# Loading half of the spectral weights two rows per partition, w_r on even and w_i on odd partitions

## The chip, the cores and the metric

The kernel runs on one core of a Trainium2 chip. The metric is the device time of one execution in microseconds (us), as the median of several runs. A run on one core counts as slow when it took over 1.5% longer than the fastest run of the same kernel. In the lines of the profile PE is TensorE's products and PEld its loading of the stationary operand, DVE is VectorE, ACT ScalarE, POOL GpSimd and SP SyncE; L12 is line 12 of the kernel. The granted clock is the share of TensorE's full speed that it was allowed in a stretch.

## The reference, cut to what matters

Attention with a decay gives x (8 batches, 576 positions, d = 512). A spectral layer follows; its weights are most of the bytes that the kernel reads (2 x 64 x 512 x 512 numbers of 4 bytes, 134 MB of the 164 MB that the profile counts).

```python
def _moe_ref(x, w_r, w_i, w_ch):            # x: (8, 576, 512); w_r, w_i: (64, 512, 512)
    X = np.fft.rfft(x, axis=1)
    Xr, Xi = np.real(X[:, :64]), np.imag(X[:, :64])
    Yr = einsum('bmd,mde->bme', Xr, w_r) - einsum('bmd,mde->bme', Xi, w_i)
    Yi = einsum('bmd,mde->bme', Xr, w_i) + einsum('bmd,mde->bme', Xi, w_r)
    ...                                      # inverse transform gives y
    u = x + y
    return u + np.maximum(u @ w_ch, 0.0)
```

## The kernel before: the parts that matter

The 64 weight tiles of 1 MiB (as written, in two-byte numbers) pass through a ring of nine buffers. All these loads are issued by GpSimd (POOL), in program order (POOL's timeline shows them so), and convert from four-byte to two-byte numbers on the way (the page counts 163.73 MB read from HBM in all, and 85.34 MB, as written, for this queue). Tiles 0 to 31 hold four modes of 128 rows of d, one row per partition; tiles 32 to 63 hold two modes of 256 rows, two rows per partition.

```python
def emit_w_load(n):
    dc, g = tile_of(n)
    if n < NTH:                                              # tiles 0..31
        wb = wpool.tile([128, 2, MG, D], BF16, tag="wb", name="wb")
        for t, src in enumerate((moe_w_r, moe_w_i)):
            pool_dma(wb[:, t, :, :],
                     src[g*MG:(g+1)*MG, dc*128:(dc+1)*128, :].rearrange("m p e -> p m e"))
    else:                                                    # tiles 32..63
        wb = wpool.tile([128, 2, M2, 2 * D], BF16, tag="wb", name="wb")
        ...  # "m (p r) e -> p m (r e)", r=2: two rows of d per partition
```

`emit_modes` multiplies a tile with X: per mode and block of 128 output columns, w_r meets the columns (Xr, Xi) and w_i meets (-Xi, Xr). These 16 columns lie side by side in `XT3[:, m, c0:c0+16]`. `emit_dft` makes XT3 from x, after each pair of batches:

```python
px = psT.tile([128, NM, 2], F32, ...)                        # 5 products into px
nc.vector.tensor_copy(_strided(XT3[:, 0, B + b:...], [[3*B, NM], [B, 2]]), px)
nc.scalar.mul(XT3[:, :, b:b+1], px[:, :, 1:2], -1.0)
```

The main loop over steps s (one head of two batches each) prefetches nine tiles, and from s = 9 on multiplies tiles, each of which frees a ring buffer and lets one more load be issued:

```python
if h == 0 and pr + STG - 1 < NPR: emit_loads(pr + STG - 1)   # k, q, v of a later pair
if s < 10 and nload < min(NRING, 3 + 3*s//4): next_w()
if s == 10: pool_dma(wch[:], ...)                            # w_ch, 0.5 MiB
...
if s >= 1 and h == 0: emit_dft(pr - 1)
if s > B:
    while nmode < (s - B) * NTH // (NS - B):
        emit_modes(nmode); nmode += 1; next_w()
```

The softmax here doesn't subtract the row's maximum and nothing guards it: scores larger than these inputs give would overflow.

## Time and profile before

| | before |
|---|---|
| time | 448.64 us (448.20 to 449.03, 3 runs) |
| profiled execution | 446.5 us |
| weights (and w_ch) in 1024-byte packets | 33,280 |
| weights in 2048-byte packets | 16,384 |
| last weight load lands | 405.3 us |

From the page of the kernel before: the span, the rows of the 40 slices for DMA (busy tenths of 16 engines, then GB/s as written), the packets, and the chain of waits by engine and by line.

```profile
span 446.5 us, 11102 instructions
...
DMA  8999999999999999999999999999999999991698
GB/s 203 206 233 233 234 234 233 152 233 206 233 234 207 234 216 224 233 211 229 231 210 235 211 212 211 211 211 211 211 211 211 211 211 211 211 196 28 225 362 296
DMA packets 66431, 97.25 MB, mean 218 GB/s; under 512 B 3376, under 2 KB 44848, under 8 KB 66384
...
DMA 58%; PE 18%; DVE 7%; ACT 7%; issue 3%; POOL 1%; SPq 1%; DVEq 0%; ACTq 0%; POOLq 0%
```

The queue is full from the second slice to the 36th, but for the eighth (152 GB/s, around 80 to 90 us). This hole can be seen closer in stretches of the kernel before (columns: stretch, its length, busy time of each engine with the count of instructions, granted clock, DMA share, GB/s), together with two stretches in which weights alone load:

```profile
78.00:80.00 2.00, 1.90 (x45) 1.70 (x45) 1.90 (x7) 1.62 (x4) 0.00 (x0) 1.00 1.01 168
80.00:81.00 1.00, 1.00 (x35) 0.97 (x31) 0.73 (x2) 0.04 (x1) 0.07 (x1) 1.00 0.28 51
81.00:82.00 1.00, 1.00 (x17) 0.65 (x15) 1.00 (x3) 1.00 (x2) 0.96 (x2) 1.00 0.11 27
82.00:83.00 1.00, 1.00 (x18) 0.76 (x17) 1.00 (x2) 1.00 (x2) 1.00 (x2) 1.00 0.63 48
...
101.00:109.00 8.00, 7.95 (x161) 6.12 (x159) 5.73 (x18) 6.48 (x10) 2.68 (x4) 0.96 1.24 206
...
300.00:400.00 100.00, 51.91 (x941) 35.70 (x939) 16.38 (x44) 12.97 (x23) 25.73 (x37) 0.69 1.12 211
```

The DMA share falls to 0.11 at 81 us. Small packets fill the queue at a share of 1.24 and large ones at 1.12: the share is the time that the packets took, summed, over the time of 16 engines, so a share above 1 only says that packets overlap, and the lower share in the second half is not an idle queue. What counts is bytes per time, and there the two forms differ by little (206 and 211 GB/s).

Why the hole is there is read from POOL's order of instructions in the kernel before (start, duration, line, what; in brackets how long POOL was idle before, and what ended that):

```profile
64.76 0.74 POOL L88 DMA_DIRECT2D wb<-in_moe_w_i_dram  x1 [1.75 <-DMA wb<-in_moe_w_r_dram]
80.93 0.74 POOL L88 DMA_DIRECT2D wb<-in_moe_w_r_dram  x1 [15.43 <-PE tp L437]
```

After nine tiles the ring is full, and POOL issues nothing for 15 us: the loads of k, q, v and w_ch that stand behind the blocked tile in program order are issued after it, at 82.43 to 84.85 us. The releaser named is TensorE's instruction that came last by the profile; in the chain of waits of the kernel before (start, duration, what) it is the products of the first tile, `A`, that end just before:

```profile
76.36 1.30 DVE XT L581 x2
...
79.87 0.76 PE A L138 x31
80.63 0.31 PE tp L437 x5
80.94 0.73 POOL wb L88
```

Two groups of the kernel before, by shape (count, busy us, mean ns, idle time before), that the change replaces in the first half:

```profile
L581 DVE CAST XT<-px 128x128 bf16<-128x128 f32 x32 | 21.0, 805 | 8.6 <-PE px L571 8.6
L585 ACT ACTIVATE XT<-px 128x64 bf16<-128x64 f32 x32 | 14.4, 466 | 18.9 <-DVE XT L581 18.0
```

(The busy time, 21.0 us over 32, is 0.66 us apiece: neighbours overlap a little.)

### The profile page before, as it was taken

Reading aid. Unit: us, or ns where it says so; the run is one execution under the profiler, and the core shown is the slowest. Engines: PE = TensorE matmul, PEld = TensorE weight load, DVE = VectorE, ACT = ScalarE, POOL = GpSimd, SP = SyncE. Lnnn points to the kernel's source line nnn. Section 1 sums busy time; section 2 is a strip of 40 time slices with the busy share of each in tenths; the row PEclk is TensorE's granted clock in tenths of the full one; section 3 lists DMA queues with packets and bytes.
Section 4 is the critical chain, followed back from the end, with each engine's and each line's share of the span. In section 5 each row is a group of like instructions: output and inputs, shape, how many; then the busy total and the mean of one; then the engine's idle time right before and its main releaser. Section 6 shows DMA issues by size and latency. Waiting matters only on the chain.

```text
span 446.5 us, 11102 instructions
## 1 busy us (share of the span) xinstructions
PE 327.1 (73%) x4791; PEld 222.6 (50%) x4791; DVE 237.3 (53%) x602; ACT 202.4 (45%) x296; POOL 146.1 (33%) x194
## 2 busy tenths in 40 slices
PE   2388888989788788768597969999822238527993
PEld 1255555766566566556465746656612224323441
DVE  5768888776676546656377664223300002103894
ACT  3378888647567454664446533443200002102442
POOL 7333330534343323323333223232322323200661
PEclk9999999959599555897769578999955558856998
DMA  8999999999999999999999999999999999991698
GB/s 203 206 233 233 234 234 233 152 233 206 233 234 207 234 216 224 233 211 229 231 210 235 211 212 211 211 211 211 211 211 211 211 211 211 211 196 28 225 362 296
DMA packets 66431, 97.25 MB, mean 218 GB/s; under 512 B 3376, under 2 KB 44848, under 8 KB 66384
## 3 DMA queue, kind: packets, MB, share of 16 engines
q0 software_dynamic: 62480, 85.34, 103.3%
q1 hardware_dynamic: 3824, 11.09, 6.9%
q8 instruction: 37, 0.61, 0.5%
q10 hardware_dynamic: 80, 0.13, 0.1%
q14 instruction: 10, 0.08, 0.0%
HBM read 163.73 MB, written 9.44 MB: 388 GB/s over the span
## 4 chain that ended last, share of the span: by engine, by line
DMA 58%; PE 18%; DVE 7%; ACT 7%; issue 3%; POOL 1%; SPq 1%; DVEq 0%; ACTq 0%; POOLq 0%
DMA wb<-in_moe_w_i_dram 30%; DMA stk<-in_k_dram 13%; DMA stq<-in_q_dram 11%; ACT E L496 4%; DMA wb<-in_moe_w_r_dram 3%; PE tp L437 3%; PE pav L534 3%; PE pxw L680 3%; PE ps L489 3%; PE A L138 2%; DVE XT L581 2%; PE vp L461 1%; DVE uo L821 1%; PE ptr L669 1%; ACT KT L450 1%
## 5 line engine op out<-in xcount | busy, mean ns | idle before, releaser
L496 ACT ACTIVATE E<-ps 128x1024 bf16<-128x1024 f32 (+1 forms) x128 | 104.5, 859 | 39.3 <-PE ps L489 27.2
L138 PE MATMUL A<-XT,wb 128*128 128x16 bf16 x2048 | 71.6, 172 | 56.8 <-DMA wb<-in_moe_w_i_dram 35.0
L138 PEld LDWEIGHTS <-wb 128*128 128x128 bf16 x2048 | 64.0, 100 | 72.6 <-DMA wb<-in_moe_w_i_dram 38.2
L88 POOL DMA_DIRECT2D wb<-in_moe_w_r_dram x65 | 47.5, 731 | 134.7 <-PE A L138 30.4
L88 POOL DMA_DIRECT2D wb<-in_moe_w_i_dram x65 | 47.1, 725 | 78.2 <-DMA wb<-in_moe_w_i_dram 45.1
L489 PE MATMUL ps<-QTs,KT 64*128 64x64 bf16 (+4 forms) x384 | 57.5, 319 | 6.1 <-ACT E L496 5.9
L534 PE MATMUL pav<-va,E 128*128 128x65 bf16 (+1 forms) x1088 | 55.9, 210 | 4.3 <-DVE x_all L556 2.6
L534 PEld LDWEIGHTS <-E 128*128 128x128 bf16 (+1 forms) x1088 | 45.1, 114 | 15.8 <-issue 5.6
L153 DVE TENSOR_TENSOR YT<-A,Yacc 128x128 bf16<-128x128 f32 x24 | 8.9, 369 | 77.2 <-PE A L138 77.2
L511 DVE TENSOR_TENSOR E<-E,trimask 128x256 bf16<-128x256 bf16 (+2 forms) x128 | 38.2, 317 | 6.8 <-ACT E L496 6.4
L450 ACT COPY KT<-tp 128x640 bf16<-128x640 bf16 (+1 forms) x32 | 22.1, 745 | 26.6 <-PE tp L437 26.4
L687 ACT CAST XW<-pxw 128x512 bf16<-128x512 f32 x36 | 20.3, 587 | 29.8 <-PE pxw L680 25.1
L680 PE MATMUL pxw<-wch,yy 128*128 128x512 bf16 x144 | 33.5, 382 | 0.0
L699 ACT CAST yy<-pyw 128x512 bf16<-128x512 f32 x8 | 4.7, 586 | 60.7 <-PE pyw L692 60.7
L437 PE MATMUL tp<-ident_bf,kb 128*128 128x128 bf16 x144 | 16.1, 269 | 19.1 <-DVE kb L421 19.1
L556 DVE TENSOR_TENSOR x_all<-pav,rcp 128x384 bf16<-128x384 f32 x64 | 29.2, 456 | 0.9
L454 ACT COPY VT<-tp 128x640 bf16<-128x640 bf16 (+1 forms) x32 | 22.5, 753 | 12.6 <-PE tp L437 12.4
L489 PEld LDWEIGHTS <-KT 64*128 64x128 bf16 x384 | 18.1, 98 | 19.8 <-issue 11.6
L828 POOL TENSOR_TENSOR uo<-uo 128x1024 f32<-128x1024 f32 x7 | 16.5, 2359 | 29.3 <-DVE uo L821 25.5
L581 DVE CAST XT<-px 128x128 bf16<-128x128 f32 x32 | 21.0, 805 | 8.6 <-PE px L571 8.6
L425 DVE TENSOR_TENSOR vb<-stv,wdec 128x1152 bf16<-128x1152 f32 x16 | 21.6, 1351 | 5.4 <-PE tp L437 4.7
L452 DVE COPY QTs<-tp 128x640 bf16<-128x640 bf16 (+1 forms) x32 | 23.3, 767 | 0.8 <-PE tp L437 0.8
(108 smaller groups left out, 439.4 us busy)
## 6 DMA issues: line engine op xcount, KB each, us to landing
wb<-in_moe_w_r_dram POOLq DMA_DIRECT2D x63, 512.0 KB, 17.6
wb<-in_moe_w_i_dram POOLq DMA_DIRECT2D x63, 512.0 KB, 18.1
out_dram<-uo SPq DMA_DIRECT2D x16, 512.0 KB, 3.7
stv<-in_v_dram POOLq DMA_DIRECT2D x14, 576.0 KB, 15.6
stk<-in_k_dram POOLq DMA_DIRECT2D x16, 288.0 KB, 15.3
stq<-in_q_dram POOLq DMA_DIRECT2D x16, 288.0 KB, 15.3
stv<-in_v_dram SPq DMA_DIRECT2D x2, 576.0 KB, 6.1
out_dram<-uo SPq DMA_DIRECT2D x7, 128.0 KB, 3.9
```

The lines of the kernel that those rows point to most:

```text
L88: tc.keep_in_program_order(nc.gpsimd.dma_start(dst, src))
L138: nc.tensor.matmul(A[:, eb, mi, :], lhsT=wb[:, t, mi, r * D + eb * 128 : r * D + (eb + 1) * 128], rhs=XT3[:, m, c0 : c0 + 2 * B], start=(i ...
L437: nc.tensor.transpose(tp[:, r - r0, :, :].rearrange("c h p -> c (h p)"), sb[:, r, :, :].rearrange("p b d -> p (b d)"), ident_bf[:, :],)
L450: nc.scalar.copy(rows(KTs[pr % 2][:, :, 0:S]), tv)
L452: nc.vector.tensor_copy(rows(QT[pr][:, :, :]), tv)
L489: nc.tensor.matmul(ps[:, b, o : o + n], lhsT=KTs[pr % 2][bs, h, jb * 128 : (jb + 1) * 128], rhs=QT[pr][bs, h, jb * 128 + c0 : jb * 128 + c ...
L496: nc.scalar.activation(E[:, :, piece * 512 : piece * 512 + w], ps[:, :, 0:w], ACT.Exp, scale=scale,)
L511: nc.vector.tensor_tensor(dg, dg, tr, ALU.mult)
L534: nc.tensor.matmul(pav[64 * half : 64 * half + w, slot, :], lhsT=E[:, b, c : c + (w - 1) * st + 1 : st], rhs=va[:, jb, b, :], start=(n == ...
L556: nc.vector.tensor_tensor(xo, pi, ri, ALU.mult)
L581: nc.vector.tensor_copy(_strided(XT3[:, 0, B + b : B + b + 1], [[3 * B, NM], [B, 2]]), px[:, :, :],)
L680: nc.tensor.matmul(pxw[:, :], lhsT=xT[:, eb, i * 128 : (i + 1) * 128], rhs=wch[:, eb, :], start=(eb == 0), stop=(eb == NDC - 1),)
```

## The change

The intent is longer packets for the first half's weights as well: 2048 bytes as written, 4 KB as read. Rows 2p and 2p+1 of d then lie in one partition, so X must lie the same way. Both w_r and w_i still have to share a tile of 128 rows of d. So w_r is put on the even partitions and w_i on the odd ones, and X is dealt to match: a copy T holds (-Xi, Xr, Xi), and four products with selection matrices put (Xr, Xi) of row 2p+r on partition 2p and (-Xi, Xr) on partition 2p+1. The number of products with the weights stays the same (2048), since each now sums over both w_r and w_i.

```diff
 # emit_w_load, n < NTH
-            wb = wpool.tile([128, 2, MG, D], BF16, tag="wb", name="wb")
+            wb = wpool.tile([128, MG, 2 * D], BF16, tag="wb", name="wb")
             for t, src in enumerate((moe_w_r, moe_w_i)):
                 pool_dma(
-                    wb[:, t, :, :],
+                    wb[t:128:2, :, :],
                     src[g * MG : (g + 1) * MG, dc * 128 : (dc + 1) * 128, :
-                    ].rearrange("m p e -> p m e"),
+                    ].rearrange("m (p r) e -> p m (r e)", r=2),
                 )
 # emit_modes, n < NTH: lhsT = wb[:, mi, r*D+es : r*D+es+128], rhs = XT3s[dc][:, r, :, m]
 # setup: two selection matrices, basis stored as [.., 2, NM] (a permuted copy)
+        for r, t in enumerate(sel):
+            nc.vector.memset(t[:, :], 0.0)
+            nc.vector.tensor_copy(_strided(t[:, 1:2], [[2, 64]]), _strided(ident_bf[:, r:r+1], [[2, 64]]))
 # emit_dft, dc < 2
+                        nc.vector.tensor_copy(T[:, 1:3, b % 2, :], px[:, :, :])
+                        nc.scalar.mul(T[:, 0, b % 2, :], px[:, 1, :], -1.0)
+                px2 = psT.tile([128, 2, 4 * NM], F32, tag="tr", name="px2")
+                for r in (0, 1):
+                    for t in (0, 1):
+                        nc.tensor.matmul(px2[:, r, :], lhsT=sel[r][:, 1 - t : 129 - t],
+                            rhs=T[:, 1 - t : 3 - t, :, :].rearrange("p c b m -> p (c b m)"),
+                            start=(t == 0), stop=(t == 1), skip_group_check=True)
+                nc.vector.tensor_copy(_strided(XT[:, 0, 2*bp, 0:1], [[2*B*NM, 2], [B*NM, 2], [1, 2*NM]]),
+                    px2[:, :, :].rearrange("p r (c n) -> p r c n", c=2))
```

(Lines are joined and cut; the XT copies of the second half only change the order in which they read.)

More of the change, by code (lines that the diff above doesn't have):

```diff
@@ L69 @@
     wch = const.tile([128, NDC, D], BF16, name="wch")
-    bas = const.tile([128, NSB + 1, NM, 2], BF16, name="bas")
+    bas = const.tile([128, NSB + 1, 2, NM], BF16, name="bas")
+    sel = [const.tile([128, 130], BF16, name=f"sel{r}") for r in range(2)]
     BI = const.tile([128, SP], BF16, name="BI")
@@ L128, in emit_modes @@
         if n < NTH:
-            terms = [(XT3s[dc], 0, t, c0) for t, c0 in ((0, B), (1, 0))]
+            terms = [
+                (lambda mi, es, r=r: wb[:, mi, r * D + es : r * D + es + 128],
+                 lambda m, r=r: XT3s[dc][:, r, :, m])
+                for r in (0, 1)
+            ]
         else:
             terms = [
-                (XT3s[2 + r], r, t, c0) for t, c0 in ((0, B), (1, 0)) for r in (0, 1)
+                (lambda mi, es, t=t, r=r: wb[:, t, mi, r * D + es : r * D + es + 128],
+                 lambda m, c0=c0, r=r: XT3s[2 + r][:, m, c0 : c0 + 2 * B])
+                for t, c0 in ((0, B), (1, 0))
+                for r in (0, 1)
             ]
@@ L136, in emit_modes @@
             for eb in range(NDC):
-                for i, (XT3, r, t, c0) in enumerate(terms):
+                for i, (w_of, x_of) in enumerate(terms):
                     nc.tensor.matmul(
                         A[:, eb, mi, :],
-                        lhsT=wb[:, t, mi, r * D + eb * 128 : r * D + (eb + 1) * 128],
-                        rhs=XT3[:, m, c0 : c0 + 2 * B],
+                        lhsT=w_of(mi, eb * 128),
+                        rhs=x_of(m),
                         start=(i == 0),
@@ L171 @@
         nrm = actx.enter_context(tc.tile_pool(name="nrm", bufs=4))
+        tpl = actx.enter_context(tc.tile_pool(name="tpl", bufs=1))
         ssb = actx.enter_context(tc.tile_pool(name="ssb", bufs=1))
@@ L277 @@
         nc.vector.tensor_copy(ident_f[:, :], ident_bf[:, :])
+        for r, t in enumerate(sel):
+            nc.vector.memset(t[:, :], 0.0)
+            nc.vector.tensor_copy(
+                _strided(t[:, 1:2], [[2, 64]]), _strided(ident_bf[:, r : r + 1], [[2, 64]])
+            )
         for t in VTs:
@@ L360, in emit_basis @@
             NB1 = NSB + 1
-            s_f = ssb.tile([128, NB1], F32, name="s_f")
+            s_f = scratch(128, NB1)
             nc.vector.tensor_copy(s_f[:], s_i[:])
-            m_f = ssb.tile([128, NM], F32, name="m_f")
+            m_f = scratch(128, NM)
             nc.vector.tensor_copy(m_f[:], m_i[:])
@@ L394, in emit_basis @@
             nc.vector.memset(Zt[0:64, 5, :, :], 0.0)
-            nc.vector.tensor_copy(bas[:, :, :, :], Zt[:, :, :, :])
+            nc.vector.tensor_copy(
+                bas[:, :, :, :], Zt[:, :, :, :].rearrange("p s m t -> p s t m")
+            )
             coef = ssb.tile([128, 1], F32, name="coef")
@@ L562, in emit_dft @@
             forms = [(dc, dc * 128, 1)] if dc < 2 else [(2, 256, 2), (3, 257, 2)]
+            if dc < 2:
+                if bp == 0:
+                    XT3s[dc] = xtpool.tile(
+                        [128, 2, 2 * B, NM], BF16, tag="XT3", name=f"XT{dc}"
+                    )
+                T = tpl.tile([128, 3, 2, NM], BF16, tag="T", name="T")
             for b in (2 * bp, 2 * bp + 1):
                 for c, d0, st in forms:
-                    if b == 0:
+                    if b == 0 and dc == 3:
                         XT3s[c] = xtpool.tile(
@@ L568, in emit_dft @@
                         )
-                    px = psT.tile([128, NM, 2], F32, tag="tr", name="px")
+                    px = psT.tile([128, 2, NM], F32, tag="tr", name="px")
                     for sb in range(NSB):
@@ L579, in emit_dft @@
                         )
+                    if dc < 2:
+                        nc.vector.tensor_copy(T[:, 1:3, b % 2, :], px[:, :, :])
+                        nc.scalar.mul(T[:, 0, b % 2, :], px[:, 1, :], -1.0)
+                        continue
                     XT3 = XT3s[c]
                     nc.vector.tensor_copy(
-                        _strided(XT3[:, 0, B + b : B + b + 1], [[3 * B, NM], [B, 2]]),
+                        _strided(XT3[:, 0, B + b : B + b + 1], [[B, 2], [3 * B, NM]]),
                         px[:, :, :],
                     )
-                    nc.scalar.mul(XT3[:, :, b : b + 1], px[:, :, 1:2], -1.0)
+                    nc.scalar.mul(
+                        _strided(XT3[:, 0, b : b + 1], [[3 * B, NM]]), px[:, 1, :], -1.0
+                    )
+            if dc < 2:
+                px2 = psT.tile([128, 2, 4 * NM], F32, tag="tr", name="px2")
+                for r in (0, 1):
+                    for t in (0, 1):
+                        nc.tensor.matmul(
+                            px2[:, r, :],
+                            lhsT=sel[r][:, 1 - t : 129 - t],
+                            rhs=T[:, 1 - t : 3 - t, :, :].rearrange(
+                                "p c b m -> p (c b m)"
+                            ),
+                            start=(t == 0),
+                            stop=(t == 1),
+                            skip_group_check=True,
+                        )
+                XT = XT3s[dc]
+                nc.vector.tensor_copy(
+                    _strided(
+                        XT[:, 0, 2 * bp, 0:1], [[2 * B * NM, 2], [B * NM, 2], [1, 2 * NM]]
+                    ),
+                    px2[:, :, :].rearrange("p r (c n) -> p r c n", c=2),
+                )
         NS = len(steps)
```

## The prediction

> **What bounds the kernel now.** The DMA queue that carries the weights. In the chain of waits 58% of the span is DMA, 30% of it w_i loads; in the 40-slice table the DMA row is at 8 or 9 until 405 us. Only the first 8 us and a hole at 80 to 83 us are not full (windows of 1 us: DMA share 0.28, 0.11, 0.63, against 1.2 when full). The 42 us tail after 405 us is output work that the change does not touch.
>
> **What the change saves.** The loads of d's first half (32 tiles of 1 MiB as written in bf16) go in 1024-byte packets; those of the second half already in 2048-byte ones. The packet records, where weights alone move, give 199.7 packets/us for the small (101 to 109 and 150 to 158 us) and 102.3 packets/us for the large (300 to 400 us). One MiB takes 5.13 us or 5.00 us: 0.124 us a tile, 4.0 us for 32 tiles if the new loads reach the second half's rate.
>
> **How much lies on the critical path.** Nine of the 32 tiles are loaded before the hole at 80 us. There the ring is full, POOL waits 15 us, and the queue runs dry until the first tile's products (PE A, in the chain at 77.7 to 80.6) free a slot. The chain from 20 to 82 us is compute (ACT E, PE, DVE). Faster loads there only widen the hole. 23 tiles remain: 2.9 us.
>
> **What the change adds, on that early compute chain.** Per pair of batches of the first half: two contiguous DVE copies px to T, estimated at 0.35 us from the BI copy of that size (0.347), instead of XT copies of 0.72; two ACT products of about 0.3 instead of 0.46; then four selection products of 256 columns (estimated 0.6 us with latency, from 128-column products at 0.25 and 512-column ones at 0.4) and one DVE copy of 128x512 out of PSUM, about 0.65 (from 0.56 for 128x384). [...] the last pair stands in the chain just before tile 0's products. I estimate 0.8 us there, 0.5 us for the earlier pairs and the prologue (two selection matrices, a permuted basis copy), and 0.2 us for products whose 16 columns now lie 128 bytes apart[...]; no such read is in the trace before. Sum: +1.5 us, all in the hole. After 90 us this is hidden behind the loads.
>
> **Sum.** 448.6 - 2.9 + 1.5 = **447.2 us, range 444.5 to 452**. Faster by over 2%: 0.03; within 2%: 0.88; slower by over 2%: 0.09.
>
> **What would show it.** Half as many weight packets before 245 us, all 2048 bytes; 209 to 210 GB/s where weights alone load in the first half; a hole at 80 us of 4 to 5 us rather than 2.5; the DVE XT group split in T (about 0.35) and XT (about 0.65); the last load at about 403 us.
>
> **What would make it wrong.** Each new load writes only even or only odd partitions. [...] then at 5% slower packets the 32 tiles would lose 8 us. If the early compute chain loses more than 3 us, the gain is eaten whole.

The sum stands as it was recorded, 448.6 - 2.9 + 1.5 = 447.2 us; what is cut from the text, and marked, are reasons that no trace or run of this case shows: one for the 0.2 us of the columns 128 bytes apart, one for the danger, and a clause on what TensorE waits for (in the profile after, TensorE's idle time before the selection products, L618, is 0.0 us). The 0.2 us is in the +1.5 (0.8 + 0.5 + 0.2), as the author's bare estimate; without it the sum would be 447.0 us. The 0.3 us for ACT's products was a bare estimate too, and the 5% of slower packets an assumption.

## The result, and the profile after

| | before | after |
|---|---|---|
| time, median | 448.83 us (448.20 to 449.25, 4 runs) | 447.75 us (447.68 to 448.02, 4 runs) |
| ratio of the fast runs | | 0.9981, 95% interval 0.9967 to 0.9995 |
| profiled execution | 446.5 us | 445.9 us |
| last weight load lands | 405.3 us | 403.9 us |

A ratio here is the mean time of one kernel's fast runs over that of the other's fast runs of the same rounds, so it is not quite the ratio of the medians that are quoted. The time fell by about 1 us, 0.2%: within 2%.

From the page after, the same lines:

```profile
span 445.9 us, 11199 instructions
...
DMA  8999999699999999999999999999999999991697
GB/s 204 210 235 238 237 236 236 108 235 210 237 237 210 237 217 230 236 217 230 235 218 230 211 211 211 211 211 211 210 212 211 211 211 211 213 186 29 226 381 270
DMA packets 50048, 97.27 MB, mean 218 GB/s; under 512 B 3376, under 2 KB 12080, under 8 KB 50000
...
PE 39%; DMA 24%; ACT 14%; DVE 10%; issue 5%; SPq 1%; POOL 1%; DVEq 0%; ACTq 0%; POOLq 0%
```

Most full slices of the first half move 1 to 6 GB/s more, and the eighth moves 108 instead of 152. The chain now runs mostly through TensorE. That is a warning about how a chain is read: the queue lost nothing between 100 and 390 us (next table), so TensorE did not become the bound there; it only ran closer behind the loads, and the chain followed it.

The same stretches of the changed kernel:

```profile
78.00:80.00 2.00, 2.00 (x31) 1.42 (x32) 1.30 (x3) 0.86 (x2) 0.00 (x0) 1.00 0.43 80
80.00:81.00 1.00, 1.00 (x20) 0.86 (x20) 0.56 (x3) 1.00 (x2) 0.00 (x0) 1.00 0.01 2
81.00:82.00 1.00, 1.00 (x31) 0.88 (x27) 0.81 (x3) 0.57 (x2) 0.00 (x0) 1.00 0.07 16
82.00:83.00 1.00, 1.00 (x22) 0.74 (x20) 1.00 (x4) 0.68 (x1) 0.80 (x1) 1.00 0.00 0
83.00:84.00 1.00, 1.00 (x17) 0.62 (x13) 0.99 (x4) 0.98 (x2) 1.00 (x3) 1.00 0.31 41
...
101.00:109.00 8.00, 7.15 (x136) 5.77 (x133) 6.69 (x18) 4.67 (x9) 2.54 (x4) 1.00 1.12 211
```

At 101 to 109 us the rate is now the 211 GB/s of the second half. The hole begins more than 1 us earlier and ends more than 1 us later. POOL after, where it is released by the first tile's products:

```profile
63.47 0.61 POOL L89 DMA_DIRECT2D wb<-in_moe_w_i_dram  x1 [1.81 <-DMA wb<-in_moe_w_r_dram]
82.20 0.81 POOL L89 DMA_DIRECT2D wb<-in_moe_w_r_dram  x1 [18.12 <-PE A L146]
```

The wait grew from 15.4 to 18.1 us, and the release moved from 80.93 to 82.20. The chain after, at the same place, now holds the selection products (L618) ahead of tile 0's products:

```profile
77.98 0.22 PE px L618
78.20 0.19 PE ps L505
78.39 0.43 PE px L618 x3
...
80.89 1.01 PE A L146 x32
```

The groups that replaced XT's copies in the first half (T, selection products, XT), after:

```profile
L603 DVE CAST T<-px 128x128 bf16<-128x128 f32 x16 | 4.0, 285 | 2.3 <-PE px L593 2.3
L604 ACT ACTIVATE T<-px 128x64 bf16<-128x64 f32 x16 | 3.1, 230 | 10.6 <-DVE T L603 10.4
L618 PE MATMUL px<-T,sel 128*128 128x256 bf16 x32 | 6.1, 310 | 0.0
L629 DVE CAST XT<-px 128x512 bf16<-128x512 f32 x8 | 5.5, 691 | 3.2 <-PE px L618 3.0
```

**A ledger of the queue.** The next table is my own count from the packet records, not a view of the profile. In all profiled runs the queue's time can be put down to packets. I counted the packets of the software queue in stretches of 10 us from 20 to 400 us in six profiles and fitted a cost of each size by least squares, leaving out stretches that were off by over 0.25 us. One packet costs the whole queue 5.006 ns (1024 bytes written), 9.776 ns (2048), 5.667 ns (1152, k and q) or 10.974 ns (4608, v). Elapsed time less the sum of these costs is time lost. All times in us, one profile each; the columns add up to the end of the last packet:

| run | packets | lost 0-70 | lost 70-130 (hole) | lost 130-395 | drain after 395 | last packet ends |
|---|---|---|---|---|---|---|
| before | 392.9 | 6.4 | 3.1 | -0.2 | 2.8 | 405.0 |
| after | 389.0 | 6.4 | 5.6 | 0.0 | 2.6 | 403.5 |
| e1 loads only | 389.0 | 6.3 | 4.3 | 0.0 | 2.4 | 401.9 |
| e2 dealing only | 392.9 | 6.2 | 4.2 | -0.1 | 2.7 | 405.9 |
| e3 contiguous columns | 389.0 | 6.2 | 8.5 | 2.3 | 2.3 | 408.3 |
| e6 halves | 389.0 | 7.6 | 4.2 | 3.3 | 5.5 | 409.6 |
| e7 w_ch early | 389.0 | 6.2 | 3.0 | 0.7 | 1.8 | 400.7 |
| e8 w_ch early, before | 392.9 | 6.2 | 1.7 | -0.2 | 2.6 | 403.2 |
| e9 w_ch, k, q, v early | 389.0 | 6.4 | 0.7 | 1.3 | 1.7 | 399.1 |
| e10 the same, before | 392.9 | 6.4 | -0.1 | -0.1 | 3.2 | 402.2 |
| e11 and x w_ch later | 389.0 | 6.2 | 0.8 | 0.5 | 2.3 | 398.7 |
| e12 the same, before | 392.9 | 6.2 | 0.0 | -0.1 | 3.3 | 402.3 |

So the change saves 3.87 us of packets and loses 2.53 us more in the hole. Single profiles of kernels that are alike up to 70 us (after, e7, e9, e11) differ by 0.2 us in the first column of losses, so differences of that size in this table show nothing. The weights are read as four-byte numbers, 2048 or 4096 bytes a packet, while v is not converted; its 4608 bytes cost 175.6 ns of an engine and a weight packet of 4096 bytes read 156.4 ns, 39 ns per kilobyte read in both. So in these runs the cost goes with the bytes read. Where weights alone load in the kernel before, at 300 to 400 us, 102.3 packets/us of 2048 bytes are 209.5 GB/s written, and so 419 GB/s read.

### The profile page after: what moved, and what is told of

Same layout as the page of the kernel before. It is cut to its first block, busy times and chain, and to the rows that moved or that the text cites. A ratio compares the mean times of both kernels' runs of the same rounds, so it can differ in the third digit from the quotient of the medians.

```text
span 445.9 us, 11199 instructions
## 1 busy us (share of the span) xinstructions
PE 330.6 (74%) x4807; PEld 230.4 (52%) x4823; DVE 240.9 (54%) x614; ACT 197.8 (44%) x296; POOL 138.2 (31%) x194
## 4 chain that ended last, share of the span: by engine, by line
PE 39%; DMA 24%; ACT 14%; DVE 10%; issue 5%; SPq 1%; POOL 1%; DVEq 0%; ACTq 0%; POOLq 0%
DMA wb<-in_moe_w_i_dram 20%; ACT E L512 10%; PE pav L550 7%; PE A L146 6%; PE ps L505 6%; PE tp L453 5%; PE pxw L729 5%; DMA stv<-in_v_dram 3%; DVE QTs L468 2%; ACT KT L466 2%; PE vp L477 2%; PE px L593 2%; PE ptr L718 1%; DVE E L527 1%; DVE XT L607 1%
## 5 line engine op out<-in xcount | busy, mean ns | idle before, releaser
L512 ACT ACTIVATE E<-ps 128x1024 bf16<-128x1024 f32 (+1 forms) x128 | 101.6, 854 | 20.1 <-PE ps L505 13.7
L89 POOL DMA_DIRECT2D wb<-in_moe_w_r_dram x65 | 43.6, 671 | 151.2 <-PE A L146 47.5
L505 PE MATMUL ps<-QTs,KT 64*128 64x64 bf16 (+4 forms) x384 | 56.4, 313 | 19.1 <-ACT E L512 18.9
L89 POOL DMA_DIRECT2D wb<-in_moe_w_i_dram x65 | 43.1, 663 | 66.5 <-DMA wb<-in_moe_w_r_dram 32.3
L550 PE MATMUL pav<-va,E 128*128 128x65 bf16 (+1 forms) x1088 | 52.7, 205 | 2.7 <-DVE va L483 1.4
L550 PEld LDWEIGHTS <-E 128*128 128x128 bf16 (+1 forms) x1088 | 43.4, 111 | 17.9 <-issue 10.8
L527 DVE TENSOR_TENSOR E<-E,trimask 128x256 bf16<-128x256 bf16 (+2 forms) x128 | 36.9, 302 | 20.5 <-ACT E L512 20.3
L729 PE MATMUL pxw<-wch,yy 128*128 128x512 bf16 x136 | 31.9, 380 | 1.4 <-issue 1.1
L561 DVE RECIPROCAL rcp<-pav 128x6 f32<-128x6 f32 x64 | 12.1, 189 | 19.6 <-PE pav L550 19.1
L729 PEld LDWEIGHTS <-yy 128*128 128x128 bf16 x144 | 13.4, 99 | 16.6 <-DVE yy L723 4.2
## 6 DMA issues: line engine op xcount, KB each, us to landing
stk<-in_k_dram POOLq DMA_DIRECT2D x16, 288.0 KB, 15.4
```

What stands on the lines that cost most here:

```text
L89: tc.keep_in_program_order(nc.gpsimd.dma_start(dst, src))
L505: nc.tensor.matmul(ps[:, b, o : o + n], lhsT=KTs[pr % 2][bs, h, jb * 128 : (jb + 1) * 128], rhs=QT[pr][bs, h, jb * 128 + c0 : jb * 128 + c ...
L512: nc.scalar.activation(E[:, :, piece * 512 : piece * 512 + w], ps[:, :, 0:w], ACT.Exp, scale=scale,)
L527: nc.vector.tensor_tensor(dg, dg, tr, ALU.mult)
L550: nc.tensor.matmul(pav[64 * half : 64 * half + w, slot, :], lhsT=E[:, b, c : c + (w - 1) * st + 1 : st], rhs=va[:, jb, b, :], start=(n == ...
L729: nc.tensor.matmul(pxw[:, :], lhsT=xT[:, eb, i * 128 : (i + 1) * 128], rhs=wch[:, eb, :], start=(eb == 0), stop=(eb == NDC - 1),)
```

## The experiments

My theory: the loads save about 3.9 us; the nine tiles that land before the hole give their share to the hole; the dealing delays the first tile's products, and so the queue's restart; after that the queue alone sets the time. Rivals are named with each run. Kernels of one call ran on one chip, with runs of the kernel before in the same rounds. The record holds no e4 or e5.

### e1: the new loads alone

```diff
 # the kernel before, with the changed emit_w_load; the products keep the old XT3
-    lhsT=wb[:, t, mi, r * D + eb * 128 : r * D + (eb + 1) * 128],
+    lhsT=wb[:, mi, t * D + eb * 128 : t * D + (eb + 1) * 128],      # n < NTH only
```

> The new loads alone; X is not dealt, so the result is wrong on purpose. My theory (the loads save 3.85 us of queue time in 32 tiles; the nine tiles that land before the hole at 80 us give theirs back to the hole; the later restart of the queue is the price of the dealing): the queue runs dry about 1.1 us earlier than in the kernel before, restarts at the same time, last load lands about 2.7 us earlier than before (405.0), time 446.0 us, ratio 0.994. Rival (the later restart comes from the loads themselves, not from the dealing): as the changed kernel, 447.7 us, ratio 0.998.

Measured: 445.57 us (445.03 to 445.76, 5 runs) beside 448.32 us of before, ratio 0.9936 (0.9925 to 0.9948). In stretches of this run the hole closes at the time of before, and begins at the time of after:

```profile
78.00:80.00 2.00, 1.91 (x50) 1.60 (x50) 0.83 (x4) 2.00 (x4) 0.00 (x0) 1.00 0.40 74
...
82.00:83.00 1.00, 1.00 (x15) 0.64 (x15) 1.00 (x4) 0.65 (x1) 1.00 (x3) 1.00 0.85 98
```

The rival (the later restart comes from the loads) falls. The loads are worth 2.75 us; of the 3.87 us of packets 1.2 us go into the hole. (The arithmetic of this kernel and of the next is wrong. The comparison with the reference passed all the same: its tolerance does not see this part of the sum.)

### e2: the dealing alone

```diff
 # the changed kernel, with the old emit_w_load for n < NTH
-    lambda mi, es, r=r: wb[:, mi, r * D + es : r * D + es + 128]
+    lambda mi, es, r=r: wb[:, r, mi, es : es + 128]
```

> The old loads with the dealing of X by selection products (wrong result on purpose). My theory: packets stay at 1024 bytes and 199.7 per us, the first tile's products end about 1.3 us later than in the kernel before (80.6), the hole grows by that, time 450.1 us, ratio 1.003. Rival (the dealing costs nothing on the path): 448.8 us, ratio 1.000.

Measured: 450.07 us (449.55 to 450.60, 5 runs), ratio 1.0041 (1.0029 to 1.0053). The dealing costs 1.75 us; the ledger has 1.2 us of that in the hole, and the last packet ends 0.9 us later. The rest, which my theory did not have, comes after the last packet (see e12). POOL is released at 81.89 us instead of 80.93. The two halves of the change add up: -2.75 and +1.75 make -1.00, and the whole change, in other rounds, measured -1.08 by the medians and -0.9 by the ratio.

### e3: the columns of a product side by side

```diff
-    [128, 2, 2 * B, NM], BF16, tag="XT3"   ...   XT3s[dc][:, r, :, m]
+    [128, 2, NM, 2 * B], BF16, tag="XT3"   ...   XT3s[dc][:, r, m, :]
-    nc.vector.tensor_copy(XT (runs of 2*NM), px2)                      # one copy of 128x512
+    for r in (0, 1):                                                   # two copies of 128x256, scattered
+        nc.vector.tensor_copy(_strided(XT[:, r, 0, 2*bp:...], [[B, 2], [1, 2], [2*B, NM]]), px2[:, r, :]...)
```

> The changed kernel with XT stored so that the 16 columns of a product lie side by side; the copy after the selection products scatters instead (two copies of 128x256 with short runs). Result correct. If the columns 128 bytes apart are the main part of the 1.3 us by which the queue restarts later: the 32 products of tile 0 take 0.75 to 0.8 us instead of 1.01, and the time falls to about 447.0 us or below. My theory says they are only 0.25 us of it, and the scattered copies cost more (estimated 1.2 us each from the old XT copy of 128x128 at 0.72, instead of one of 0.69): time 448.5 to 449.5 us, ratio about 1.000.

Measured: 452.74 us (452.25 to 454.13, 5 runs), ratio 1.0102 (1.0089 to 1.0115): the direction of my theory, but 3 us beyond its range. The products of tile 0, in the time order of TensorE of this run, took 0.93 us for 31; the changed kernel's 32 took 1.17 us in the same view. So columns 128 bytes apart cost about 0.2 us at this tile, as estimated, and are not the main part. (Over the later tiles of the first half it is less: back to back, products start 30 ns apart on average in the changed kernel and 26.6 ns in this run, about 0.1 us a tile.) What was mis-sized is the scattering: the group of copies in this run is

```profile
L630 DVE CAST XT<-px 128x256 bf16<-128x256 f32 x16 | 18.7, 1346 | 3.4 <-PE px L618 3.4
```

1.35 us each and two a pair, 2.7 us instead of 0.69. POOL was released at 84.98 us, the hole took 8.5 us, and the queue lost another 2.3 us between 290 and 313 us. Storing XT in long runs and reading it with gaps, as the change does, is the better side of that trade here (0.2 us at tile 0 against 2.0 us a pair).

### e6: w_r on the lower half, w_i on the upper half

```diff
-    wb[t:128:2, :, :],
+    wb[64 * t : 64 * t + 64, :, :],
-    lhsT=sel[r][:, 1 - t : 129 - t],              # sel is 130 wide, ones at columns 1, 3, ...
+    lhsT=sel[r][:, 64 - 64 * t : 192 - 64 * t],   # sel is 192 wide, ones at columns 64 to 127
```

> The changed kernel with w_r on partitions 0 to 63 and w_i on 64 to 127 (correct result)[...]. [...] where weights alone load in the first half the packets fall from 102 per us[...], time 452 to 457 us. If they do not[...]: 102 per us and 447.7 us as the changed kernel. [...]

Fewer packets/us and 452 to 457 us: I leaned to it 60 to 40; "If they do not" is the other case, in which the choice of partitions does not matter.

Measured: 453.08 us, the median of four fast runs (451.62 to 457.79), ratio 1.0125 (1.0086 to 1.0164); two runs at 458.52 and 461.67 count as slow by the 1.5%, though at granted clocks (0.795, 0.797) within those of the fast ones (0.780 to 0.800). The time is in the range forecast, but the rate did not fall where weights alone load in the first half: at 101 to 109 us this run moved 101.9 packets/us, as many as after (both 211 GB/s in that stretch of the profile). The loss comes in spells. By the ledger, against after, 1.2 us are lost before 70 us, 3.3 us at 130 to 395 us (most of it between 180 and 250 us) and 2.9 us more in the drain after 395 us, where only the unchanged loads of the second half are left; the hole is 1.4 us smaller. Two of the spells:

```profile
60.00:66.00 6.00, 4.68 (x74) 3.33 (x75) 5.51 (x18) 4.61 (x7) 2.17 (x4) 1.00 1.16 199
...
240.00:250.00 10.00, 6.56 (x108) 4.96 (x105) 5.75 (x17) 5.70 (x9) 4.28 (x6) 0.84 1.11 205
```

(the changed kernel moved 213 and 211 there), and from run to run by different amounts: its fast runs spread over 6 us, those of e9 over 3 us and those of every other kernel here over less than 2 us. Shown is that the choice of partitions alone is worth about 1.4% (1.0125 over the changed kernel's 0.9981, from different rounds) and steady times; even and odd partitions cost nothing that can be seen against 128 (102.1 packets/us against 102.3). Why the partitions matter no run shows, and why the loss comes in spells is open.

### e7 and e8: w_ch into the hole

```diff
-            if s == 10:
+            if s == 9:                      # ahead of the tile that waits for the first products
                 pool_dma(wch[:], ...)
```

e7 is the changed kernel with this, e8 the kernel before with it.

> The changed kernel with the load of w_ch issued one step earlier, ahead of the tile that waits for the first products, so that it goes into the hole at 80 us. If the hole is time lost for good (my theory: the queue is the bound from 84 us on), its 512 packets of 1024 bytes (2.56 us of queue time) are taken out of the later stream: 445.0 us, ratio 0.993. If the time is set by the compute chain that the changed kernel's chain of waits shows from 100 to 313 us (rival), nothing is gained: 447.5 us, ratio 0.998.

> The same move of w_ch in the kernel before: its hole of 3.0 us takes 2.56 us of load: 445.8 us, ratio 0.994. Rival (compute sets the time): 448.3 us.

Measured: e7 444.96 us (444.44 to 445.72, 5 runs), ratio 0.9921 (0.9909 to 0.9933), as my theory had it: the 2.56 us came out of the stream, so the chain through TensorE in the page after was no bound. e8 447.54 us (446.60 to 448.45, 6 runs), ratio 0.9977 (0.9963 to 0.9992): only 1.1 us of 2.5. Its profiled run shows where some of it went: the hole shrank to 1.0 us, but the queue ran short again at 97 to 99 us (0.7 us), waiting for products. Its two slowest runs had granted clocks of 0.776 and 0.803 against 0.820 and 0.793 of its two fastest, so the clock does not settle it. My size for e8 was wrong, and the rest of its loss is open.

### e9 and e10: k, q and v of the next pair too

```diff
-            if h == 0 and pr + STG - 1 < NPR:
-                emit_loads(pr + STG - 1)
+            if s == 9 or (h == 0 and s != 10 and pr + STG - 1 < NPR):
+                emit_loads((s + 1) // 2 + STG - 1)
```

with the move of w_ch; e9 on the changed kernel, e10 on the kernel before.

> The changed kernel with both the w_ch load and the k, q, v loads of the next pair (5 us of queue time) issued ahead of the waiting tile. My theory: the hole (5.6 us lost in all) is filled whole, 441.9 us, ratio 0.986. Rival (compute behind the queue takes over once the loads run 5 us ahead): 443.5 to 445 us, with new dry spells between 260 and 330 us, where the queue waits for the first half's products.

> The same two moves in the kernel before: its hole of 3.1 us is filled: 445.2 us, ratio 0.993. With both holes filled the change should be worth its full 3.85 us of packet time, against 1 us as it stands: the ratio of the run before this one to this one 0.991 to 0.993.

Measured: e9 444.58 us (443.35 to 446.59, the five fast runs; one slow at 451.80), ratio 0.9918 (0.9898 to 0.9938). e10 445.88 us (445.44 to 446.47, 5 runs), ratio 0.9940 (0.9928 to 0.9952). The hole at 80 us is gone in both (e9 still loses 0.6 us at 95 to 100 us); the k, q and v of one pair take 4.3 us by the ledger's costs, where I had 5. But the change is worth only 0.9918 / 0.9940 = 0.9978 between the two, about 1 us as before, where I had expected 0.991 to 0.993: that expectation failed. For the rival was right about e9: with the loads 4.9 us ahead (5.6 less 0.7 in the ledger) the queue waits for TensorE at another place. In stretches of e9 the hole is full at 257 GB/s, while at 280 to 300 us TensorE is busy without a gap and the rate is down from 211 to 198:

```profile
78.00:84.00 6.00, 6.00 (x115) 4.56 (x113) 4.67 (x15) 4.63 (x7) 1.42 (x2) 1.00 1.16 257
280.00:300.00 20.00, 20.00 (x265) 12.37 (x263) 5.74 (x16) 8.97 (x16) 5.73 (x8) 1.00 1.10 198
```

In its chain of waits the x times w_ch products stand there, between the products of two tiles:

```profile
281.77 0.71 PE A L146 x29
282.49 0.91 PE ptr L718 x16
283.40 3.63 PE pxw L729 x16
```

### e11 and e12: those products eight tiles later

```diff
-                if nmode % 4 and nx < B:
+                if nmode > NTH + 7 and nmode % 4 and nx < B:
                     emit_xw(nx)
```

on top of e9 and of e10.

> The changed kernel with both early loads and, in the second half, the x times w_ch products (16 transposes or more and as many products of 512 columns after each of the first tiles) begun eight tiles later. In the run with the early loads alone the queue lost 1.3 us at 284 to 297 us while TensorE was busy without a gap and the ring waited for its products. If those products are what the queue waits for there: no dry spell between 260 and 330 us, 442.3 us, ratio 0.986. Rival (any further time is lost elsewhere, such as to the granted clock): 444.6 us, ratio 0.992, as with the early loads alone.

> The kernel before with the same three moves, to see what the change is worth when neither hole nor TensorE hides it. The kernel before lost nothing in this stretch with the early loads alone (445.9 us), so 445.5 to 445.9 us, ratio 0.994; the run before this one over this one 0.992, which is 3.85 us of packet time less about 0.5.

Measured: e11 443.10 us (442.62 to 443.33, 4 runs), ratio 0.9871 (0.9856 to 0.9886): the fastest of all, 5.8 us under the kernel before in the same rounds and about 4.9 under the changed kernel by the ratios (0.9871 over 0.9981, from different rounds). The same stretch in e11:

```profile
280.00:300.00 20.00, 19.46 (x285) 12.93 (x289) 6.59 (x17) 7.55 (x13) 5.71 (x8) 0.96 1.12 211
```

The dry spell is gone, as expected; the time stayed 0.8 us above what I expected. e12: 445.52 us (445.20 to 445.87, 5 runs), ratio 0.9929 (0.9916 to 0.9941). The change is then worth 0.9871 / 0.9929 = 0.9942, which is 2.5 us (445.53 less 443.04, the means of the fast runs), against 1 us as it stands and 0.992 expected; the last packet ends 3.6 us earlier (398.7 against 402.3). The missing 1 us is after the loads: from the last packet to the end of the last store the profile of e12 takes 39.7 us and that of e11 41.3; 39.9 before, 40.7 after.

The other profiles narrow this down. The five without the dealing (before, e1, e8, e10, e12) take 39.7 to 40.3 us there, the seven with it (after, e2, e3, e6, e7, e9, e11) 40.4 to 41.4, 0.8 us more on average. So the longer tail goes with the dealing and not with the new loads: e1 has them and takes 40.3, e2 lacks them and takes 40.5. TensorE's last product is not later (it starts 34.1 to 34.7 us after the last packet in both groups), so the time goes in the last stores. Why is not shown: no run was made for it.

## Why the prediction was right

**The sum.** Predicted 447.2 us (444.5 to 452), measured 447.75; predicted gain 1.4 us, measured 1.1 by the medians and 0.9 by the ratio. Up to the end of the loads the sum held: the last packet ended 1.4 us earlier (405.0 to 403.5), and the last load landed at 403.9 us (predicted about 403). After that the tail took some of it back.

**The packets.** Predicted 0.124 us a tile, 4.0 us for 32; the ledger has 3.87. The new loads ran at the second half's rate: 102.1 packets/us at 101 to 109 us. The reason that twice as long packets bring so little is in the fitted costs: 1024 bytes take an engine 80.1 ns (16 times 5.006) and 2048 bytes 156.4 ns. A straight line through these two, an estimate, gives 76.3 ns for each kilobyte written and only 3.8 ns for each packet.

**The part that is off the path.** Predicted 1.1 us (nine of 32 tiles); e1 shows 1.2 us more hole.

**The price of the dealing.** Predicted 1.5 us, all in the hole: 0.8 for the last pair, 0.5 for the earlier pairs and the prologue, 0.2 for the columns. The restart moved by 1.27 us (80.93 to 82.20) in the two profiles shown, and e2 shows 1.2 us more hole. "All in the hole" was wrong: e2 lost 1.75 us in time, and the rest goes with the longer tail. The parts can be read from all the profiles (e3, with its other copies, left out). The prologue shows no delay: the first transposes of the chain start at 19.64 to 20.22 us in the six with the dealing and at 19.70 to 20.17 in the five without. From there to the first product with x of the last pair takes 0.4 us longer (55.0 to 55.3 against 54.6 to 55.0), and from that to the end of tile 0's products 0.5 us longer (6.4 against 5.8 to 6.0), the columns included. That is 0.9 us in all where 1.5 was predicted, and the 0.8 for the last pair was more than twice too large. Of the single instructions, the T copies took 0.285 us (0.35 predicted), ACT's 0.23 (0.3), the last copy 0.69 (0.65), and the columns 128 bytes apart 0.2 us at tile 0 (0.2). That the sum for the hole came so near is in part luck.

**The hole.** Predicted 4 to 5 us instead of 2.5; by the ledger 5.6 instead of 3.1. The growth of 2.5 us was predicted (1.1 + 1.5); the starting value, read from three windows of 1 us, was too small, because the queue thins out at 79 us already.

**The danger named.** The even and odd loads were not slower (102.1 packets/us against 102.3). e6 shows that another natural choice of partitions does cost time: 453.08 us, ratio 1.0125.

**What was missed.** The tail ("output work that the change does not touch"): the span fell less than the loads did (0.6 against 1.4 us in the two profiles), and the tail was longer in every profile with the dealing, by 0.8 us on average (e12). Against a gain of 1.4 us this is no small term; the range was wide enough to hide it. And several sizes in my later expectations (e3, e8, e9, and what the change is worth between e10 and e9) were wrong.

## What to carry to other kernels

Before counting what faster loads bring, look for stretches where the queue is dry already: what was saved before such a hole only widened it here (1.2 of 3.87 us, e1), and what was added to the compute that ends the hole was paid in full (POOL released 0.96 us later and 1.2 us more hole in the ledger, e2). A hole in front of a full ring is better filled with loads that need no ring buffer, by moving them ahead of the blocked one in the issuing order (here worth more than the change itself: 0.9940 in e10 against 0.9981). And when loads are split over partitions, the interleaved split cost nothing that can be seen here (102.1 packets/us against 102.3), while the split into halves cost over 1% and made the time unsteady (451.62 to 457.79 us in the fast runs of e6).
